# Loads of k in 1 KB runs with a GpSimd copy, and other durations in the plan of an attention and expert kernel

## The chip, the cores and the metric

The kernel runs on one core of one Trainium2 chip. Its engines are TensorE (PE in the rows, its weight loads PEld), VectorE (DVE), ScalarE (ACT), GpSimd (POOL) and SyncE (SP, which here only issues transfers). The metric is the device time of one execution in microseconds; lower is better.

## The reference

Three stages follow each other, all in float32.

```python
# 1. attention over a window of 64 positions; q, k, v are (4 batches, 8 heads, 576, 64)
scores = q @ k^T / 8, masked to 0 <= i - j < 64
attn = exp(scores - max);  attn /= sum(attn) + 1e-9
x = (attn @ v) as (2304 tokens, 512)
# 2. eight experts, each token goes to the best one
logits = x @ w_gate + modality_bias[modality_id];  e = argmax(logits)
out[token] = gate_weight * (relu(x @ w1[e]) @ w2[e])          # 512 -> 1024 -> 512
# 3. one dense layer; w_in, w_out are float64
h = out @ w_in                                                # 512 -> 2048
y = (h - tanh(h)) @ w_out
```

## The kernel before

**Stages.** The attention works on 16 head pairs (four per batch, numbered 0 to 15) of 512 positions, and on one tail unit per batch with the last 64 positions of its eight heads. For a pair, SP loads k, q and v; PE transposes k and q into PSUM (L549, L554), DVE or ACT copies them to SBUF, PE forms the scores of both heads (L642 puts the mask into the bank, L655 adds q times k), DVE takes the row maxima (L722), ACT the exponentials with their sums (L725), DVE the reciprocals (L728, L729), POOL mostly the product (L731). PE transposes the result (L680), ACT and DVE copy it out, and PE multiplies by v (L694). POOL also makes vb, a copy of v that is moved by half a tile (L478, L479), and the small kTt copies (L583).

**Routing.** After each batch a chain of small DVE operations with some PE work assigns its tokens to experts (L833 to L953). It needs the gate weights, which SP loads (L521, tile eqa) and DVE prepares (L525 to L534). Gated rows go to DRAM (L816).

**Experts.** Two units of 504 tokens are known early (after batches 0 and 2), three more when all batches are routed. Each is gathered (L1189), transposed (L1207), split into two fp32r parts (xh and xl, L1220), and goes through two layers of matmuls (L1282, then L1302), each as high times high, high times low and low times high. The weights come in 16 tiles per unit (L1233, L1239), are copied to wh and split off to wl (L1257) by DVE, the first two units' also by POOL. Beside it the float64 words of w_in and w_out are converted to float32 and split, tile by tile (L1378 to L1399 on DVE, L1393 and L1386 on POOL). From about 345 us on the dense layer runs (L1686, L1732).

**What sets the order.** Every instruction is put out by a planner, `Flow`. Each step of work is a generator that yields an `Op` with an engine (or several to choose from), a duration in us, what it waits for, a ring of buffers and a PSUM bank. The planner keeps a clock for each engine and one for the transfers (`wire`), picks what can start first, ties by priority, and writes the engines' instruction streams in that order once, at build time. At run time each engine goes through its stream in order and waits on semaphores. A changed duration moves instructions, though not what is computed. `Bag` is a set of buffers, some lent from the conversion's tiles (craw) until a given pair.

**The load of a pair.** A partition of the tile takes four neighbouring positions c of both heads h. It is laid out c, h, d so that one transposition takes both heads' 64 columns, which makes each run of the transfer one row of 64 floats (256 bytes). The two tiles of a pair live in one place of the bag qk: two of its own and three lent ones.

Of the kernel before, what the change touches and what calls it, by code (L numbers as in the profile page):

```python
# [8 lines left out]
F32 = mybir.dt.float32  # L9
# [23 lines left out]
NEARLY = 2  # L33
# [18 lines left out]
NWA = 3  # L52
DQ = 0.62
# [188 lines left out]
class Kernel:  # L242
# [132 lines left out]
    def front(self):  # L375
# [20 lines left out]
        R["qk"] = Bag(qk, [self.lend_qk() for i in range(3)], LEND - 1)  # L396
# [34 lines left out]

    def lend_qk(self):
        t = self.cv.tile([128, 1024], I32, name="craw", bufs=3).bitcast(F32)
        t = t.rearrange("p (x c h d) -> p x c h d", x=2, c=4, h=2)
        return t[:, 0], t[:, 1]

    def load_qk(self, pi, qk, qe=None):
# [4 lines left out]
        for t, src in ((k, "k"), (q, "q")):  # L442
            eng = nc.sync if src == "k" or qe is None else qe
            eng.dma_start(  # L444
                t, ap[src][b, h0 : h0 + 2, 0:512, :].rearrange("h (p c) d -> p c h d", c=4),
            )
        self.raw["qk", pi] = (q, k)

    def t_load(self):
        nc, ap, at, R = self.nc, self.ap, self.at, self.rings  # L450

        def qk(pi):
            r = yield Op(("SP", DQ if pi == 0 else 1.7), rings=[R["qk"].ask(pi)], prio=1.25 * pi - 2, wire=2.4)
# [3 lines left out]
            self.tk("qk", pi).t = r.t  # L457

        def tail(b):
            r = yield Op(("SP", 1.7), rings=[R["tl"]], prio=5 * b, wire=1.2)  # L460
# [6 lines left out]
        def v(pi):  # L467
            b, hp = divmod(pi, 4)
            h0 = 2 * hp
            r = yield Op(("SP", 1.3), rings=[R["va"]], prio=1.25 * pi + 0.3, wire=1.2)  # L470
# [11 lines left out]
        def vtail(b):  # L482
            r = yield Op(("SP", 1.3), rings=[R["vt"]], prio=5 * b + 2, wire=1.1)
# [53 lines left out]
    def t_prep(self):  # L537
        nc, R = self.nc, self.rings
        for pi in range(4 * B):
            b, hp = divmod(pi, 4)  # L540
            base = 5 * b + hp - 0.75
            q, k = self.raw["qk", pi] if ("qk", pi) in self.raw else (None, None)
            r = yield Op(("PE", 0.45), [self.tk("qk", pi)], [R["kT"].ask(pi)], bank=self.bankA | self.bankX, prio=base)
            self.raw["kTr", pi] = r.rel[0]
            self.raw["T", pi] = r.rel[0].x
            q, k = self.raw["qk", pi]
# [4 lines left out]
            r = yield Op(("PE", 0.45), bank=self.bankA | self.bankX, prio=base)  # L551
            pq, bq = self.bt(r, 128, 4, 128), r.bt
            for c in range(4):
                nc.tensor.transpose(pq[:, c, :], q[:, c].rearrange("p h d -> p (h d)"), self.idF)  # L554
            self.raw["qkr", pi].t = r.t
# [160 lines left out]
    def t_soft(self, key, ps, P, bs, tok):  # L716
# [6 lines left out]
        r = yield Op(("ACT", 1.25), [r.tok])  # L723
# [3 lines left out]
        r = yield Op(("DVE", 0.3), [r.tok])  # L727
# [97 lines left out]
    def route(self, b):  # L825
# [36 lines left out]
        r = yield Op(("DVE", 0.8))  # L862
# [172 lines left out]
    def unit_table(self, tc):  # L1035
# [29 lines left out]
        r3 = yield Op(("DVE", 3.0))  # L1065
# [181 lines left out]
    def t_wsplit(self, i, s, w, tok, rel):  # L1247
# [6 lines left out]
        by = dict(DVE=0.72, POOL=1.1) if i < NEARLY else dict(DVE=0.72)  # L1254
# [103 lines left out]
    def t_conv(self, n, t):  # L1358
        nc, cv, R = self.nc, self.cv, self.rings
        yield Op(None, [self.tk("w", *t), self.tk("O", CONV0), Tok(CONVT + CONVP * n)])  # L1360
        yield Op(None, [t for b in ("qk", "kT", "P") for t in R[b].back()])
# [524 lines left out]
```

## Time and profile before

| what | value |
|---|---|
| median of 3 runs | 765.63 us (765.39 to 768.44) |
| the profiled execution | 763.43 us, its span 761.3 us |
| busy in the span | PE 96%, DVE 83%, ACT 68%, POOL 40% |
| chain that ended last | PE 80%, DVE 9%, issue 3%, ACT 2%, DMA 2%, SP queue 2% |
| PE busy in 0 to 93 us | 78.96 of 93 us |
| PE busy in 140 to 205 us | 61.02 of 65 us |
| PE busy in 205 to 345 us | 140.00 of 140 us |

The chain that ended last is followed back from the last instruction; its shares say which engine the end waited for, summed over the whole span. The stages differ: the attention fills roughly the first 93 us, attention and the first expert units share 93 to 205 us, experts alone run to 345 us, the dense layer after that. A busy PE is not a PE at its peak, since the ends of matmuls are modelled; how long the same work takes in another stretch says more.

### The profile page before, as it was taken

How to read it: one execution, taken by the hardware profiler on the slowest of the kernel's cores; microseconds unless marked ns; L12 is line 12 of the kernel's file. 1: busy time of each engine (PE TensorE's matmuls, PEld its weight loads, DVE VectorE, ACT ScalarE, POOL GpSimd, SP SyncE). 2: the span in 40 equal slices, each digit the busy share in tenths (PEclk: the TensorE clock that was granted, in tenths of full speed). 3: DMA queues.
4: the chain of work that ended last, by engine and by line, in shares of the span. 5: the costliest groups of instructions: out<-in, count | busy, mean ns of one | idle time of the engine just before them, and what ended most of it. 6: DMA issues, size and time to landing. Idle time of an engine off the chain costs nothing.

```text
span 761.3 us, 14216 instructions
## 1 busy us (share of the span) xinstructions
PE 729.1 (96%) x4940; PEld 630.5 (83%) x4940; DVE 628.5 (83%) x1112; ACT 519.5 (68%) x1226; POOL 303.8 (40%) x322
## 2 busy tenths in 40 slices
PE   7898899999899999998999999999999999999994
PEld 4687677778688887897999989899999999898982
DVE  5799887889988978556998988888898888889883
ACT  4689777647656556448897777677767777776761
POOL 4556543233442422118694433234243324423221
PEclk9999999999999999999999999999999999999998
DMA  9989935668787774651010100001010001001001
GB/s 157 192 197 226 219 98 146 193 186 252 216 269 220 228 250 167 202 154 29 2 43 1 42 21 22 14 29 42 1 43 22 21 5 39 22 0 43 1 0 46
DMA packets 129462, 77.28 MB, mean 102 GB/s; under 512 B 67764, under 2 KB 122548, under 8 KB 129382
## 3 DMA queue, kind: packets, MB, share of 16 engines
q1 hardware_dynamic: 122502, 66.38, 32.1%
q0 software_dynamic: 3264, 9.63, 4.3%
q8 instruction: 41, 0.67, 0.4%
q10 hardware_dynamic: 3616, 0.28, 0.4%
q14 instruction: 39, 0.32, 0.1%
HBM read 62.10 MB, written 14.16 MB: 100 GB/s over the span
## 4 chain that ended last, share of the span: by engine, by line
PE 80%; DVE 9%; issue 3%; ACT 2%; DMA 2%; SPq 2%; POOL 0%; DVEq 0%; POOLq 0%; ACTq 0%
PE ps_g L1686 25%; PE ps_q L1732 25%; PE bank L1302 13%; PE bank L1282 10%; DVE wl L1257 1%; PE bank L1207 1%; PE bank L694 1%; DMA kr<-in_k 1%; PE bank L655 1%; SPq L444 1%; ACT P L725 1%; PE bank L680 1%; DMA eqa<-in_wg 1%; DVE rhs L933 1%; PE bank L833 1%
## 5 line engine op out<-in xcount | busy, mean ns | idle before, releaser
L1717 POOL TENSOR_TENSOR gl<-gv,gh 128x384 fp32r<-128x384 f32 x94 | 100.7, 1071 | 166.4 <-ACT gh L1716 166.1
L1708 DVE COPY_PREDICATED gv<-gm,gt 128x384 f32<-128x384 int32 x96 | 110.7, 1153 | 10.2 <-ACT gu L1698 0.5
L1732 PE MATMUL ps_q<-H,gl 128*128 128x512 f32 x288 | 113.3, 396 | 0.2 <-DVE gl L1717 0.2
L1732 PE MATMUL ps_q<-H,gh 128*128 128x512 f32 x288 | 113.0, 392 | 0.0
L1716 ACT ACTIVATE gh<-gv 128x384 fp32r<-128x384 f32 x96 | 50.2, 523 | 89.2 <-issue 77.8
L1704 DVE SCALAR_TENSOR_TENSOR gv<-gu,ps_g 128x384 f32<-128x384 f32 x96 | 52.9, 551 | 40.1 <-ACT gt L1701 39.6
L1706 DVE SCALAR_TENSOR_TENSOR gv<-gs,gv 128x384 f32<-128x384 f32 x96 | 77.3, 805 | 3.3
L1257 DVE TENSOR_TENSOR wl<-raw,wh 128x512 fp32r<-128x512 f32 x76 | 69.7, 933 | 10.9 <-ACT wh L368 10.1
L1732 PEld LDWEIGHTS ps_q<-H,gl 128*128 128x128 f32 x288 | 54.0, 188 | 12.7 <-DVE gl L1717 0.6
L1705 DVE SCALAR_TENSOR_TENSOR gv<-gs,gv 128x384 f32<-128x384 f32 x96 | 60.2, 627 | 3.3
L1700 ACT ACTIVATE gs<-gu,pa 128x384 f32<-128x384 f32 x96 | 57.9, 604 | 6.4 <-DVE gv L1706 6.4
L1699 ACT ACTIVATE gs<-gu,pa 128x384 f32<-128x384 f32 x96 | 59.3, 618 | 3.5 <-DVE gv L1705 0.3
L1732 PEld LDWEIGHTS ps_q<-H,gh 128*128 128x128 f32 x288 | 54.1, 188 | 8.8
L1703 ACT ACTIVATE gm<-gu,pth 128x384 f32<-128x384 f32 x96 | 58.1, 605 | 0.0
L1707 DVE TENSOR_TENSOR gt<-ps_g,gt 128x384 f32<-128x384 f32 x96 | 52.6, 548 | 0.0
L1698 ACT ACTIVATE gu<-ps_g 128x384 f32<-128x384 f32 x96 | 45.4, 473 | 0.0
L1701 ACT ACTIVATE gt<-ps_g 128x384 f32<-128x384 f32 x96 | 45.1, 470 | 0.0
L725 ACT ACTIVATE P<-bank,nm 128x128 f32<-128x128 f32 x104 | 37.3, 400 | 10.9 <-DVE nm L722 10.7
L368 ACT ACTIVATE ys<-bank 128x504 f32<-128x504 f32 (+1 forms) x20 | 11.1, 556 | 47.4 <-PE bank L1302 29.9
L1282 PE MATMUL bank<-xl,wh 128*128 128x504 f32 (+1 forms) x160 | 41.8, 378 | 0.0
L1282 PE MATMUL bank<-xh,wh 128*128 128x504 f32 (+1 forms) x160 | 40.8, 374 | 0.0
L1282 PE MATMUL bank<-xh,wl 128*128 128x504 f32 (+1 forms) x160 | 40.5, 373 | 0.0
(454 smaller groups left out, 2035.5 us busy)
## 6 DMA issues: line engine op xcount, KB each, us to landing
raw<-in_w SPq DMA_DIRECT2D x80, 256.0 KB, 4.0
craw<-in_win SPq DMA_DIRECT2D x16, 512.0 KB, 5.1
craw<-in_wout SPq DMA_DIRECT2D x16, 512.0 KB, 4.0
va<-in_v SPq DMA_DIRECT2D x32, 128.0 KB, 5.0
yd<-ys SPq DMA_DIRECT2D x16, 252.0 KB, 4.1
yr<-yd SPq DMA_DIRECT2D x20, 192.0 KB, 2.4
kr<-in_k SPq DMA_DIRECT2D x10, 256.0 KB, 4.9
qr<-in_q SPq DMA_DIRECT2D x9, 256.0 KB, 5.9
```

The costliest lines, as they stand in the source:

```text
L1257: self.eng(r).tensor_tensor(lo, w, hi.bitcast(F32), op=ALU.subtract)
L1282: nc.tensor.matmul(ps, wt[:, k, :], xt[:, k, :n], start=(k == 0 and q == 0), stop=(k == 3 and q == 2))
L1302: nc.tensor.matmul(ps, wt[:, k % 4, :], h, start=(q == 0), stop=(q == 3 * NF1 - 1))
L1686: nc.tensor.matmul(ps, w[:, c, :], x[:, c, :], start=(c == 0 and i == 0), stop=(c == 3 and i == 2))
L1699: nc.scalar.activation(s1, u, AF.Square, bias=self.pa1)
L1700: nc.scalar.activation(s2, u, AF.Square, bias=self.pa2)
L1703: nc.scalar.activation(m, u, AF.Relu, bias=self.pth)
L1705: nc.vector.scalar_tensor_tensor(v, s1, b1, v, op0=ALU.add, op1=ALU.mult)
L1706: nc.vector.scalar_tensor_tensor(v, s2, b2, v, op0=ALU.add, op1=ALU.mult)
L1708: nc.vector.copy_predicated(v, m.bitcast(I32), t)
L1717: (nc.vector if last else nc.gpsimd).tensor_tensor(gl, v, gh.bitcast(F32), op=ALU.subtract)
L1732: nc.tensor.matmul(self.po[t], g[:, t * 128 : t * 128 + 128], w, start=(f == 0 and i == 0), stop=(f == NF2 - 1 and i == 2),)
```

## The change

For k of pairs 1 to 10 (`PACK`) the transfer now writes a partition's 512 floats in the order h, c, d. A run is then four positions of one head, 256 floats or 1 KB, and the load has 256 runs in place of 1,024. GpSimd copies the tile into the order c, h, d in another tile (`t_pack`, line 465 of the changed file), and PE transposes from there. q, v, the tails and k of the other pairs stay as they were. The two buffers for the copies (bag qp) are cut from one of the three lent places of qk, which keeps two. The other edits are numbers of the plan: transfer times by run length (`W256`, `W1K`), and durations of the exponentials, of the reciprocals, of two routing steps on DVE and of the weight splits. The diff, cut to its core (where a line is changed in the same way in several places, one stands):

```diff
@@ constants
+W256, W1K = 1.34, 0.77
+PACK = {("k", pi) for pi in range(1, LEND - 1)}
@@ front()
-        R["qk"] = Bag(qk, [self.lend_qk() for i in range(3)], LEND - 1)
+        R["qk"] = Bag(qk, [self.lend_qk() for i in range(2)], LEND - 1)
+        R["qp"] = Bag([], [t.rearrange("p (c h d) -> p c h d", h=2, c=4) for t in self.lend_flat()], LEND - 1)
...
+    def lend_flat(self):
+        t = self.cv.tile([128, 1024], I32, name="craw", bufs=3).bitcast(F32)
+        return t[:, 0:512], t[:, 512:1024]
...
@@ load_qk()
-            eng.dma_start(
-                t, ap[src][b, h0 : h0 + 2, 0:512, :].rearrange("h (p c) d -> p c h d", c=4),
-            )
+            x = ap[src][b, h0 : h0 + 2, 0:512, :]
+            if (src, pi) in PACK:
+                t = t.rearrange("p c h d -> p (c h d)").rearrange("p (h c d) -> p h c d", h=2, c=4)
+                eng.dma_start(t, x.rearrange("h (p c) d -> p h c d", c=4))
+            else:
+                eng.dma_start(t, x.rearrange("h (p c) d -> p c h d", c=4))
...
+    def t_pack(self, pi, n, tok):
+        new, to = self.tk("qp", n, pi), self.raw["qk", pi]["qk".index(n)]
+        if (n, pi) in PACK:
+            r = yield Op(dict(POOL=0.8), [tok], [self.rings["qp"].ask(pi)], prio=1.25 * pi - 1)
+            x = to.rearrange("p c h d -> p (c h d)").rearrange("p (h c d) -> p c h d", h=2, c=4)
+            to = r.rel[0].x
+            self.nc.gpsimd.tensor_copy(to, x)
+        else:
+            r = yield Op(None, [tok])
+        self.raw["qp", n, pi] = to, r.rel
+        new.t = r.t
@@ t_load(): the planner's transfer times
-            r = yield Op(("SP", DQ if pi == 0 else 1.7), rings=[R["qk"].ask(pi)], prio=1.25 * pi - 2, wire=2.4)
+            r = yield Op(("SP", DQ if pi == 0 else 1.7), rings=[R["qk"].ask(pi)], prio=1.25 * pi - 2, wire=sum(W1K if (n, pi) in PACK else W256 for n in "qk"))
...
+            for n in "kq":
+                self.flow.add(self.t_pack(pi, n, r.tok), 1.25 * pi - 1)
-            r = yield Op(("SP", 1.7), rings=[R["tl"]], prio=5 * b, wire=1.2)
+            r = yield Op(("SP", 1.7), rings=[R["tl"]], prio=5 * b, wire=W256)
...
@@ t_prep(): the transposes wait for the packed tile
-            r = yield Op(("PE", 0.45), [self.tk("qk", pi)], [R["kT"].ask(pi)], bank=self.bankA | self.bankX, prio=base)
+            r = yield Op(("PE", 0.45), [self.tk("qp", "k", pi)], [R["kT"].ask(pi)], bank=self.bankA | self.bankX, prio=base)
...
-            q, k = self.raw["qk", pi]
+            k, rk = self.raw["qp", "k", pi]
...
+            for t in rk:
+                t.t = r.t
@@ planner's durations
-        r = yield Op(("ACT", 1.25), [r.tok])
+        r = yield Op(("ACT", 1.37), [r.tok])
...
-        r = yield Op(("DVE", 0.3), [r.tok])
+        r = yield Op(("DVE", 0.36), [r.tok])
...
-        r = yield Op(("DVE", 0.8))
+        r = yield Op(("DVE", 1.1))
...
-        r3 = yield Op(("DVE", 3.0))
+        r3 = yield Op(("DVE", 4.5))
...
-        by = dict(DVE=0.72, POOL=1.1) if i < NEARLY else dict(DVE=0.72)
+        by = dict(DVE=0.8, POOL=1.2) if i < NEARLY else dict(DVE=0.8)
@@ t_conv(): a lent buffer more to wait for
-        yield Op(None, [t for b in ("qk", "kT", "P") for t in R[b].back()])
+        yield Op(None, [t for b in ("qk", "qp", "kT", "P") for t in R[b].back()])
```

Since the planner writes the streams anew, instructions move on all engines. In the changed file the lines have other numbers: 465 is the new copy, 502 and 503 make vb, 549 to 558 prepare the gate, 599 and 591 copy kT and qT, 611 makes kTt, 644 copies the tail's k, 750 takes the maxima, 756 and 757 are the reciprocals, 759 is the product, 372 the copies, 1248, 1285 and 1344 make xl, wl and hl, 1406 to 1427 convert.

First place, DVE's stream around the preparation of the gate (eqa is the loaded gate weight, nm the maxima, smm and rc the sums and reciprocals, PT the transposed product). Before:

```order
L571 COPY kT_104<-bank_465 128x4x2x64
L728 TENSOR_SCALAR smm<-smm 128x4
L729 RECIPROCAL rc<-smm 128x4
L616 COPY kTt_86<-bank_496 128x4x64
L525 COPY wgp<-eqa 128x4x8
...
L534 TENSOR_TENSOR btok<-btok,ob 128x160
L722 TENSOR_REDUCE nm<-bank_535 128x4
L722 TENSOR_REDUCE nm<-bank_536 128x4
L370 COPY PT<-bank_591 128x512
```

And now:

```order
L757 RECIPROCAL rc<-smm 128x4
L644 COPY kTt_86<-bank_495 128x4x64
L372 COPY PT<-bank_508 128x512
L549 COPY wgp<-eqa 128x4x8
...
L558 TENSOR_TENSOR btok<-btok,ob 128x160
L756 TENSOR_SCALAR smm<-smm 128x4
L757 RECIPROCAL rc<-smm 128x4
L750 TENSOR_REDUCE nm<-bank_538 128x4
L750 TENSOR_REDUCE nm<-bank_539 128x4
L750 TENSOR_REDUCE nm<-bank_597 128x4
L599 COPY kT_106<-bank_613 128x4x2x64
```

The preparation keeps its place, before the maxima of pair 3. One copy of a product moved ahead of it, and one pair of reciprocals (pair 2, second head) moved behind it.

Second place, POOL's stream from the product of pair 1 to that of pair 2 (vb is the copy of v, cva and cvr are lent buffers of products). Before:

```order
L731 TENSOR_TENSOR P_113<-P_113,rc 128x512
L731 TENSOR_TENSOR P_114<-P_114,rc 128x512
L478 COPY vb<-va 64x384
L479 COPY vb<-va 64x384
L731 TENSOR_TENSOR cva<-cva,rc 128x512
L731 TENSOR_TENSOR cvr<-cvr,rc 128x512
L583 COPY kTt_86<-kT_104 128x64
```

And now, where `craw<-kr` is the new copy:

```order
L759 TENSOR_TENSOR P_113<-P_113,rc 128x512
L759 TENSOR_TENSOR P_114<-P_114,rc 128x512
L502 COPY vb<-va 64x384
L503 COPY vb<-va 64x384
L611 COPY kTt_86<-kT_104 128x64
L759 TENSOR_TENSOR cva<-cva,rc 128x512
L465 COPY craw<-kr_97 128x512
L465 COPY craw<-kr_99 128x512
L759 TENSOR_TENSOR cvr<-cvr,rc 128x512
```

The copies of k of pairs 4 and 5 stand between the two products of pair 2.

Third place, DVE's stream just ahead of the third expert unit's first xl. Before:

```order
L1378 TENSOR_SCALAR cva<-cva 128x512
L1316 SCALAR_TENSOR_TENSOR hl_133<-bank_3447,hh_125 128x504
L1257 TENSOR_TENSOR wl<-raw,wh 128x512
L1340 CAST pif<-ids_2471 126x4
L1380 TENSOR_SCALAR cva<-cva 128x512
L1382 SCALAR_TENSOR_TENSOR cva<-craw,cva 128x512
L1316 SCALAR_TENSOR_TENSOR hl_134<-bank_3474,hh_126 128x504
L1257 TENSOR_TENSOR wl<-raw,wh 128x512
L1220 TENSOR_TENSOR xl<-bank_3513,xh 128x504
```

And now:

```order
L1344 SCALAR_TENSOR_TENSOR hl_133<-bank_3415,hh_125 128x504
L1285 TENSOR_TENSOR wl<-raw,wh 128x512
L1368 CAST pif<-ids_2503 126x4
L1408 TENSOR_SCALAR cva<-cva 128x512
L1410 SCALAR_TENSOR_TENSOR cva<-craw,cva 128x512
L1344 SCALAR_TENSOR_TENSOR hl_134<-bank_3445,hh_126 128x504
L1248 TENSOR_TENSOR xl<-bank_3483,xh 128x504
```

The last split of a weight tile went behind xl. Counted from the start of the stream to that first xl, DVE has 24 weight splits and 10 converted tiles (L1378) before, and 21 and 6 now; two of the splits went to POOL, the rest comes later.

## Rows read from the trace of the kernel before

**Rows 1.** Busy time by stretch: us, engines' busy time, PE clock, DMA share, GB/s

```profile
10.00:60.00 50.00, 43.76 (x777) 35.91 (x775) 40.82 (x117) 38.11 (x162) 27.29 (x41) 0.97 0.98 195
30.00:40.00 10.00, 9.55 (x182) 8.21 (x183) 8.42 (x20) 7.68 (x38) 5.89 (x10) 0.83 1.04 197
175.00:204.00 29.00, 26.69 (x123) 21.48 (x122) 28.73 (x45) 21.20 (x40) 9.43 (x7) 1.00 0.77 223
```

**Rows 2.** Transfers of 8 to 23 us, then of 165 to 175 us

```profile
DMA packets 11881, 2.85 MB, mean 190 GB/s; under 512 B 11879, under 2 KB 11879, under 8 KB 11879
...
DMA packets 3019, 3.12 MB, mean 312 GB/s; under 512 B 176, under 2 KB 2838, under 8 KB 3018
```

**Rows 3.** SP's queue in time; issue times (ns shortest/median/longest); us to landing

```profile
21.16 1.06 SPq L521 DMA_DIRECT2D eqa<-in_wg  x1
22.88 0.61 SPq L444 DMA_DIRECT2D kr<-in_k  x1
...
L444 SPq DMA_DIRECT2D kr<-in_k x10: 607/959/4162, 0.8 to 88.8; - x10
...
L1407 SPq DMA_DIRECT2D craw<-in_win x16: 374/382/1588, 135.3 to 233.8; - x16
...
kr<-in_k SPq DMA_DIRECT2D x10, 256.0 KB, 4.9
```

**Rows 4.** DVE in order of time: start, us, line; in brackets idle time before

```profile
23.03 0.39 DVE L616 COPY kTt<-bank 128x256 f32<-128x256 f32 x1
26.44 0.18 DVE L525 COPY wgp<-eqa 128x32 f32<-128x32 f32 x1 [3.02 <-DMA eqa<-in_wg]
...
27.89 1.28 DVE L722 TENSOR_REDUCE nm<-bank 128x4 f32<-128x512 f32 x2
```

**Rows 5.** PE in order of time, from pair 4's transposes on

```profile
27.55 0.60 PE L554 MATMUL bank<-idF,craw 128*128 128x128 f32 x4
29.87 0.34 PE L694 MATMUL bank<-PT,va 128*64 128x64 f32 x4 [1.72 <-issue]
...
32.03 1.12 PE L549 MATMUL bank<-idF,kr 128*128 128x128 f32 x4
...
34.36 1.11 PE L655 MATMUL bank<-kT,qT 64*64 64x128 f32 x32
35.30 0.38 PE L642 MATMUL bank<-mF,idB 64*64 64x512 bf16 x2
...
37.12 0.66 PE L549 MATMUL bank<-idF,kr 128*128 128x128 f32 x4
```

**Rows 6.** POOL in order of time, then DVE's sums at the same time

```profile
25.49 0.24 POOL L583 COPY kTt<-kT 128x64 f32<-128x64 f32 x1
29.86 0.50 POOL L478 COPY vb<-va 64x384 f32<-64x384 f32 x1 [4.13 <-DMA va<-in_v]
...
41.45 1.04 POOL L731 TENSOR_TENSOR P<-P,rc 128x512 f32<-128x512 f32 x1 [0.77 <-DVE rc L729]
...
41.63 0.89 DVE L728 TENSOR_SCALAR smm<-smm 128x4 f32<-128x4 f32 x1 [0.32 <-ACT P L725]
```

**Rows 7.** The chain of waits, 175 to 248 us: start, us, what

```profile
175.74 2.75 PE bank L1282 x12
...
203.89 0.65 PE bank L1207 x4
...
225.91 21.97 PE bank L1282 x96
```

**Rows 8.** DVE by line, 175 to 204 us: count, busy us, mean ns

```profile
L1257 DVE TENSOR_TENSOR wl<-raw,wh 128x512 fp32r<-128x512 f32 x10 | 11.3, 1133 | 0.0
...
L1382 DVE SCALAR_TENSOR_TENSOR cva<-craw,cva 128x512 int32<-128x512 int32 x7 | 4.8, 691 | 0.2
L1380 DVE TENSOR_SCALAR cva<-cva 128x512 int32<-128x512 int32 x7 | 3.9, 559 | 0.1
L1378 DVE TENSOR_SCALAR cva<-cva 128x512 f32<-128x512 f32 x6 | 2.5, 416 | 0.0
```

More of the change, by code (lines that the diff above doesn't have):

```diff
@@ L469, in v @@
             h0 = 2 * hp
-            r = yield Op(("SP", 1.3), rings=[R["va"]], prio=1.25 * pi + 0.3, wire=1.2)
+            r = yield Op(("SP", 1.3), rings=[R["va"]], prio=1.25 * pi + 0.3, wire=W256)
             va = at.tile([128, 4, 2, 64], F32, name="va", bufs=NVA)
@@ L482, in vtail @@
         def vtail(b):
-            r = yield Op(("SP", 1.3), rings=[R["vt"]], prio=5 * b + 2, wire=1.1)
+            r = yield Op(("SP", 1.3), rings=[R["vt"]], prio=5 * b + 2, wire=W256)
             nc.sync.dma_start(self.vt, ap["v"][b, :, 448:576, :].rearrange("h p d -> p h d"))
@@ L541, in t_prep @@
             base = 5 * b + hp - 0.75
-            q, k = self.raw["qk", pi] if ("qk", pi) in self.raw else (None, None)
-            r = yield Op(("PE", 0.45), [self.tk("qk", pi)], [R["kT"].ask(pi)], bank=self.bankA | self.bankX, prio=base)
+            r = yield Op(("PE", 0.45), [self.tk("qp", "k", pi)], [R["kT"].ask(pi)], bank=self.bankA | self.bankX, prio=base)
             self.raw["kTr", pi] = r.rel[0]
             self.raw["T", pi] = r.rel[0].x
-            q, k = self.raw["qk", pi]
+            k, rk = self.raw["qp", "k", pi]
             pk, bk = self.bt(r, 128, 4, 128), r.bt
@@ L550, in t_prep @@
             self.flow.add(self.t_kcopy(pi, pk, bk, r.tok), base)
-            r = yield Op(("PE", 0.45), bank=self.bankA | self.bankX, prio=base)
+            for t in rk:
+                t.t = r.t
+            r = yield Op(("PE", 0.45), [self.tk("qp", "q", pi)], bank=self.bankA | self.bankX, prio=base)
+            q, rk = self.raw["qp", "q", pi]
             pq, bq = self.bt(r, 128, 4, 128), r.bt
@@ L554, in t_prep @@
                 nc.tensor.transpose(pq[:, c, :], q[:, c].rearrange("p h d -> p (h d)"), self.idF)
+            for t in rk:
+                t.t = r.t
             self.raw["qkr", pi].t = r.t
```

## The prediction

> **What bounds the kernel now.** I read the busy time by stretch first, then the transfers, then DVE, PE and POOL in order of time around the stalls, and last the chain of waits from 175 us on. PE does the same matmuls before and after, so what can be won is time in which PE waits or runs slowly, and that lies ahead of 204 us. Two places hold a good part of it.
>
> The first is at 22 to 36 us. Up to 60 us the transfer engines are full, at a share of 0.98 and 195 GB/s [rows 1], and from 8 to 23 us all but two of the packets are under 512 B [rows 2]. In that queue stands the gate weight, issued at 21.16 us behind the q, k and v of four pairs [rows 3]. DVE ends its work at 23.42 us and stands still for 3.02 us until that weight lands; what is queued behind it, the maxima of pair 3, starts at 27.89 us [rows 4]. PE then stands still for 1.72 us ahead of pair 2's last product, and the chip grants it a lower clock: 0.83 on average in 30 to 40 us [rows 1], so in part the lower of its two levels, 1.2 GHz in place of 2.4. Four transposes take 1.12 us at 32.03 us and 0.66 us at 37.12 us [rows 5].
>
> The second is at 175 to 204 us. PE starts the second expert unit's first layer at 175.74 us and goes on to the next unit's transposes at 203.89 us, 28.15 us later. The same 96 matmuls of the next unit take 21.97 us [rows 7]. So 6.2 us are lost, and DVE is the reason: busy for 28.73 of 29 us [rows 1], with weight splits of 1,133 ns and conversions of 416 to 691 ns [rows 8].
>
> **The change part by part.**
>
> *Ten loads of k.* A load of 256 KB takes 1.38 us at 190 GB/s. With packets mostly from 512 B to 2 KB the same engines moved 312 GB/s, that is 0.84 us [rows 2]. The difference is 0.54 us a load, and four of the ten loads stand ahead of the gate weight: 2.2 us. If SP's issuing were the pace and not the bytes, the difference would be that of the shortest issues, 0.607 against 0.374 us [rows 3], 0.9 us for four. If neither is, it is nothing. I take 2.2 us, since the engines are full there, and keep 0. The six later loads end nobody's wait that I found in these rows; I count them at nothing, hidden under loads that run well ahead of their use, and if that cover is gone each is worth its 0.5 us.
>
> The Trainium skill has another price ("DMA: Bandwidth & Descriptors", section "Why small descriptors are slow (HBM only)"): a fixed cost of about 3 cycles on top of 8 for a packet of 256 B, 27% by its words. By that alone a run of 1 KB would save about a fifth of 1.38 us, an estimate of 0.29 us a load and 1.1 us for four, and the sum below would come out about 1.1 us higher. The rows' 190 against 312 GB/s say more than that, with other packet sizes and another mix.
>
> *The gate and what is behind it.* The weight lands at 24.2 us instead of 26.44. DVE still waits for it: of what moved, one copy came ahead and one pair of reciprocals went behind, about 0.2 us in all. The preparation takes 1.45 us (26.44 to 27.89) and ends at 25.7. Behind it now come pair 2's last reciprocal and then its product on POOL. That product also stands behind two of the new copies, the second of which needs k of pair 5. This load was issued at 22.88 us, now about 2.2 us earlier, and lands 4.9 us after that [rows 3], at 25.6. So POOL starts the product at about 26.2 either way and ends at 27.2, with 1.04 us for it [rows 6]. PE then has 24 transposes and the scores of pair 4 ahead, by the pace at full clock (four transposes in about 0.5 us between starts, the scores in 0.94 us from 34.36 to 35.30 [rows 5]) some 3.1 us with the masks. Pair 4's scores end at about 30.3, against 35.30 before; most of pair 2's last product now comes after them, an estimate of 1.4 of the 2.16 us between its start at 29.87 and 32.03 us. That is 3.6 us won: 2.2 from the data, about 1 from the clock, the rest from the order. PE's wait for the product stays, so the clock may fall again: I take 3.0 us, with 0 and 3.7 as ends.
>
> *Ten copies on POOL.* The trace has no such copy. Its copies take 0.24 us for 64 elements a partition and 0.50 us for 384 [rows 6], which goes on to 0.61 us for 512; the product, with two inputs, takes 1.04. Ten copies make 6.1 us, at most 10.4. POOL is busy for 27.29 of the 50 us to 60 us [rows 1], so there is room. The copy adds its length to the way from a landed k to its transposition; where the load is early enough this costs nothing. What it can cost is DVE: the small sum at 41.63 us takes 0.89 us and ends at 42.52, together with POOL's product (41.45 plus 1.04) [rows 6]. Most of DVE's time goes to reads of PSUM, so I let two of ten copies strike, each with about 0.25 us, and take 0.5 us; the ends are 0 and 6.1.
>
> *The buffers.* One of three lent places for q and k goes, so loads run four pairs ahead instead of five. SP's next load into a place waits for the transposes of q four pairs before; pair 5 takes the place that pair 1 left. Nothing by these rows, under a microsecond if the first batch's loads stall.
>
> *The plan's durations.* They cost no time themselves; they move work. Two things are seen in the order. First, ahead of the third unit's first split DVE has 3 weight splits and 4 converted tiles less. By the means in [rows 8] that is 3.4 us plus 4 x 1.67 us, 10.1 us less. Against this stand six more copies that DVE takes over from ScalarE, 3.8 us by the 0.64 us of one maximum [rows 4], which reads as many elements. Net about 6 us less in the stretch in which DVE makes PE wait for 6.2. The removed work comes later, where PE was busy all the time and DVE had room. Second, the routing of the last batch comes later: 88 of the first unit's 96 first-layer matmuls stand ahead of it, 50 before. So its DVE chain falls between the first units' splits, which takes back a part. I take half of the 5 us that seem sure, 2.5 us, with 0 and 6.2 as ends.
>
> **The sum.** 763.43 - 3.0 - 2.5 + 0.5 = 758.4 us for an execution like the profiled one, whose span is 761.3 us with 2.1 us around it. The median of the runs shown, 765.63, lies 2.2 us above the profiled one, so the forecast for the median is 760.6 us. Rearranged work elsewhere I put at 0, give or take 1.5 us.
>
> **The rivals.**
>
> *Given back.* The early gain is real, but PE only reaches the stretch at 175 us sooner and waits there for DVE, whose stream has the routing of the last batch in it. For: DVE was busy for 28.73 of 29 us. Against: DVE too stands still for less time early on. Both terms then come to nothing but half a microsecond: 765.1 us.
>
> *Both in full.* 3.7 and 6.2 us, no lock: 755.7 us. For: the stalls stand in the rows. Against: DVE would have to be no bound anywhere.
>
> *Slower: GpSimd becomes the bound from 8 to 60 us.* Place: POOL's stream, where each copy waits for its k, and a product of probabilities or a vb waits behind it. Each vb wait of this kind was as long as 4.13 us [rows 6]. If every copy delays a product on the path by 0.61 to 1.04 us, that is 6.1 to 10.4 us, less the 2.2 us of the loads: 4 to 8 us, and a time of about 770 us. It decides from the point at which products start over 0.6 us later after their reciprocals, on average, than now. Against: POOL has 22.7 us free, and four units are in work at a time. By the Trainium skill ("SBUF — State Buffer", section "Who interferes with whom") a GpSimd instruction and certain DVE instructions exclude each other for the whole length of one, which makes the lock of up to 0.61 us a copy part of this case; the row at 41.63 us agrees.
>
> *The loads get no quicker.* What paces them is then not the packets: half a microsecond of copies on DVE, and the later stretch as it may be: 764.5 us.
>
> **How the numbers follow.** The forecast 0.43 (its own range 758.5 to 763), given back 0.24, both in full 0.12, GpSimd 0.16, loads no quicker 0.05. Half a percent, 3.8 us, is about what a measurement of this kernel tells from no change: the bounds are 761.8 and 769.5. Faster: three quarters of the forecast, the full case and a little of the third, 0.48. Slower: the GpSimd case, 0.16. Same: 0.36. The range from 755.5 to 769.5 us leaves out most of the GpSimd case and half of the full one.
>
> **What would show it.** In the profile after: the wait ahead of the gate's preparation under 1.5 us and its start before 25 us; k loads with packets of 1 KB and more than 200 GB/s until 30 us; POOL's copies near 0.6 us; the scores of pair 4 ending before 32.5 us; the second unit's first layer in under 26 us. The forecast is wrong if the gate still lands after 26 us, if PE's waits ahead of the transposes of products grow, or if the layer still takes 28 us.

## The result, and the profile after

The changed kernel took 758.46 us (median of 7 runs, 755.77 to 761.83), the kernel before 766.83 us beside it (764.91 to 768.84): a ratio of 0.9895, with an interval of 0.987 to 0.992, or 8 us. The forecast was 760.6 us, worked out from the 765.63 us of the three runs that were shown. The profiled execution took 756.57 us, its span 754.7 us, against 763.43 and 761.3 us before. PE's share of the chain that ended last rose from 80% to 88%, DVE's fell from 9% to 5%.

Busy time by stretch in the changed kernel, the columns as in [rows 1]:

```profile
10.00:60.00 50.00, 45.24 (x837) 37.31 (x836) 44.06 (x124) 42.04 (x183) 34.64 (x52) 1.00 0.92 210
30.00:40.00 10.00, 10.00 (x247) 8.20 (x240) 9.74 (x22) 8.51 (x44) 7.57 (x12) 1.00 0.88 208
175.00:204.00 29.00, 29.00 (x137) 23.76 (x136) 26.73 (x48) 19.37 (x37) 11.18 (x10) 1.00 0.81 234
```

In all three PE waits less than in [rows 1]. The granted clock in 30 to 40 us is 1.00 in place of 0.83, DVE is busy for 26.73 us of the 29 in which it was busy for 28.73, and the transfers of the first stretch run at 210 GB/s. Those of 8 to 23 us, to be held against the first of [rows 2], are in a tenth of their packets longer than 512 B and run at 212 GB/s:

```profile
DMA packets 10153, 3.18 MB, mean 212 GB/s; under 512 B 9149, under 2 KB 10149, under 8 KB 10149
```

In order of time (start, us, engine and line, in brackets the idle time before and what ended it), the gate weight, its preparation and pair 2's product, which stood in [rows 3 to 6]:

```profile
18.91 0.69 SPq L545 DMA_DIRECT2D eqa<-in_wg  x1
...
22.44 0.41 DVE L549 COPY wgp<-eqa 128x32 f32<-128x32 f32 x1 [0.33 <-DMA eqa<-in_wg]
22.77 0.60 POOL L465 COPY craw<-kr 128x512 f32<-128x512 f32 x1
22.77 0.63 DVE L551 CAST obp<-obp 128x20 f32<-128x20 int32 x1
24.22 0.33 DVE L556 TENSOR_TENSOR btok<-obp,rhs 128x160 f32<-128x160 f32 x1 [0.60 <-DMA rhs<-in_mb]
25.00 0.61 POOL L465 COPY craw<-kr 128x512 f32<-128x512 f32 x1 [1.63 <-PE bank L771]
25.05 0.58 DVE L756 TENSOR_SCALAR smm<-smm 128x4 f32<-128x4 f32 x1
25.77 1.86 DVE L750 TENSOR_REDUCE nm<-bank 128x4 f32<-128x512 f32 x3
26.00 1.04 POOL L759 TENSOR_TENSOR cvr<-cvr,rc 128x512 f32<-128x512 f32 x1 [0.38 <-DVE rc L757]
27.09 0.46 PE L708 MATMUL bank<-idF,cvr 64*128 64x64 f32 x8 [0.68 <-POOL cvr L759]
29.74 1.10 PE L683 MATMUL bank<-kT,qT 64*64 64x128 f32 x32
...
34.20 1.04 PE L683 MATMUL bank<-cvw 64*64 64x128 f32 x32
```

The weight is issued 2.25 us earlier and DVE waits for it for 0.33 us in place of 3.02. Pair 4's scores end at 30.84 us; before they ended at 35.47 (34.36 plus 1.11 [rows 5]).

The chain of waits from 171 to 246 us, which answers to [rows 7]:

```profile
171.21 7.79 PE bank L1310 x34
...
179.10 14.38 PE bank L1310 x62
...
193.94 1.29 PE bank L1235 x12
...
217.31 21.97 PE bank L1310 x96
```

This chain follows what the end waited for. It isn't a list of what PE lost, so PE's own rows have to stand beside it, before and then after:

```profile
152.73 0.65 PE L1207 MATMUL bank<-idF,xg 126*128 126x126 f32 x4 [1.67 <-DVE T L953]
...
175.57 1.07 PE L1282 MATMUL bank<-xh,wh 128*128 128x504 f32 x4
...
197.55 0.62 PE L1302 MATMUL bank<-hh,wh 128*128 128x504 f32 x2
198.00 1.45 PE L1207 MATMUL bank<-idF,xg 126*128 126x126 f32 x12
...
203.89 0.65 PE L1207 MATMUL bank<-idF,xg 126*128 126x126 f32 x4 [2.14 <-DVE xl L1220]
...
206.25 3.05 PE L1302 MATMUL bank<-hl,wh 128*128 128x504 f32 x8
```

```profile
171.05 1.07 PE L1310 MATMUL bank<-xh,wh 128*128 128x504 f32 x4
...
193.32 0.62 PE L1330 MATMUL bank<-hh,wh 128*128 128x504 f32 x2
193.77 1.46 PE L1235 MATMUL bank<-idF,xg 126*128 126x126 f32 x12
...
244.37 0.65 PE L1235 MATMUL bank<-idF,xg 126*128 126x126 f32 x4 [1.50 <-DVE xl L1248]
```

The second unit's first layer runs through in both kernels, in some 22 us, and so it does in every kernel below (22.1 to 22.6 us). What changed lies ahead of it and behind it. Before, PE waited 1.67 us for the routing's table T and 2.14 us for the next unit's xl, and after that second wait the granted clock was 0.72 in 204 to 210 us, so in part at the lower level: eight matmuls took 3.05 us there, and 2.00 at other places. Both waits are gone. The fourth unit's xl is now late instead, by 1.50 us at 244.37 us; the clock stays at 1.00 behind it. The 28.15 us of [rows 7] run to the last four of the sixteen transpositions of the next unit. Taken in this way the stretch is 28.3 us before and 25.4 now, and where an expectation below gives the length of the second unit's first layer, this stretch is meant.

**A measure for all kernels below.** All of them do the same matmuls, in different orders. So I took PE's time at a mark, less the matmuls that stand ahead of the mark in its stream at their full pace: 0.229 us for 504 columns (21.97 us by 96) and about as much for 512, 0.108 us for a transposition (1.29 us by 12), 0.03 us for the small ones. What is left is the time that PE has lost so far, good to some 0.7 us, since the prices are rough and a trace can lack some matmuls. *Front* is that loss at the first transposition of the second expert unit (some 150 us), *late* what is added until the last one of the fourth unit (some 250 us). Both are worked out from single profiled executions; the ratio is from timed runs, each against the kernel before on the same chip. On the chip of e5, e7, e8 and t_134 the kernel before took 762.41 us, on the others 766.83 to 768.48, and the changed kernel was not timed on the first; a ratio of these four and one of the others can differ by the chip alone. *Ahead* is the number of converted tiles that DVE has ahead of the third unit's first xl.

| kernel | k loads | durations | transfer times | ahead | front | late | ratio (interval) |
|---|---|---|---|---|---|---|---|
| before | 256 B | old | old | 10 | 49.8 | 6.6 | 1 |
| changed | 1 KB | new | new | 6 | 47.0 | 2.5 | 0.9895 (0.987 to 0.992) |
| e3_short_runs | 256 B | new | new | 6 | 53.6 | 2.4 | 0.9931 (0.9913 to 0.9949) |
| e4_double_copy | 1 KB, copies twice | new | new | 6 | 48.0 | 2.4 | 0.9879 (0.9862 to 0.9897) |
| e9_after_shift | 1 KB | new | new | 6 | 49.4 | 2.4 | 0.9892 (0.9871 to 0.9914) |
| e12_gather_late | 1 KB | new | new | 6 | 51.7 | 2.4 | 0.9863 (0.983 to 0.9896) |
| t_134 | 1 KB | new | new | 6 | 50.6 | 3.3 | 0.995 (0.9929 to 0.9972) |
| e11_old_wires | 1 KB | new | old | 8 | 58.4 | 3.6 | 0.9987 (0.9969 to 1.0005) |
| e10_old_durations | 1 KB | old | new | 10 | 54.4 | 7.8 | 0.9973 (0.9952 to 0.9994) |
| e2_pack_only | 1 KB | old | old | 10 | 56.2 | 7.9 | 1.0042 (1.0023 to 1.0061) |
| e8_pack_shift | 1 KB | old | old | 10 | 48.1 | 8.8 | 1.0042 (1.0025 to 1.006) |
| e1_plan_only | 256 B | new | new | 6 | 55.9 | 3.1 | 0.9994 (0.9975 to 1.0013) |
| e7_plan_shift | 256 B | new | new | 6 | 48.7 | 2.6 | 0.9962 (0.9941 to 0.9982) |
| e5_conv_late | 256 B | old | old | 6 | 49.2 | 4.4 | 1.004 (1.0024 to 1.0055) |

*Late* falls into two groups: 6.6 to 8.8 us with the old durations, 2.4 to 3.6 us with the new ones. Between them, at 4.4 us, lies e5, which has the old durations but only 6 tiles ahead. It is steady: 2.4 or 2.5 us in the five kernels with the changed kernel's streams and due times. *Front* goes from 47.0 to 58.4 us and follows no single edit. In these five it goes from 47.0 to 53.6. The profiled execution of e10_old_durations took 4.5 us more than that kernel's median, that of e11_old_wires 3.1 more, that of the changed kernel 1.9 less, so one execution can't rank fronts that are a few us apart.

### The profile page after: what moved, and what is told of

The parts are those of the page before. It is cut to its first block, busy times and chain, and to the rows that moved or that the text cites. A ratio compares the mean times of both kernels' runs of the same rounds, so it can differ in the third digit from the quotient of the medians.

```text
span 754.7 us, 14255 instructions
## 1 busy us (share of the span) xinstructions
PE 726.0 (96%) x4940; PEld 627.6 (83%) x4940; DVE 631.4 (84%) x1110; ACT 521.2 (69%) x1225; POOL 316.4 (42%) x335
## 4 chain that ended last, share of the span: by engine, by line
PE 88%; DVE 5%; issue 2%; ACT 2%; POOL 1%; DMA 1%; SPq 0%; POOLq 0%; ACTq 0%; DVEq 0%
PE ps_g L1714 26%; PE ps_q L1760 25%; PE bank L1310 14%; PE bank L1330 13%; PE bank L683 2%; PE bank L722 2%; PE bank L1235 1%; ACT P L753 1%; PE bank L708 1%; PE bank L524 1%; PE bank L833 1%; PE bank L861 1%; PE bank L670 1%; DMA rhs<-in_mb 1%; DVE nm L750 1%
## 5 line engine op out<-in xcount | busy, mean ns | idle before, releaser
L1285 DVE TENSOR_TENSOR wl<-raw,wh 128x512 fp32r<-128x512 f32 x74 | 65.4, 900 | 8.0 <-ACT wh L370 6.7
L370 ACT ACTIVATE wh<-raw 128x512 fp32r<-128x512 f32 x70 | 42.8, 630 | 1.6 <-DMA raw<-in_w 1.4
```

What stands on the lines that cost most here:

```text
L1285: self.eng(r).tensor_tensor(lo, w, hi.bitcast(F32), op=ALU.subtract)
```

## The experiments

**The run length alone (e3_short_runs).** The changed kernel with k loaded in rows, and the same copies:

```diff
-            if (src, pi) in PACK:
+            if False:
...
-            x = to.rearrange("p c h d -> p (c h d)").rearrange("p (h c d) -> p c h d", h=2, c=4)
+            x = to
```

> The changed kernel's very order, with GpSimd's ten copies, but k arrives in rows of 256 bytes, already in the order for the transposition; only the length of the runs is undone. Theory: the gate weight lands about 2 us later than with 1 KB runs, near 24.5 us, pair 4's scores end 2 to 3 us later, and the time is 2 to 3 us above the changed kernel's: ratio to before 0.993. Rival 1 (run length does nothing; SP's place in the queue and the plan do it all): same as the changed kernel, 0.989. Rival 2 (loads carry all): 1.000.

Measured: 0.9931, against 0.9895; 0.0036 of 767 us are 2.8 us, and the two intervals leave 0.4 to 5.1 us. Against the next kernel, e4, which ran on the same chip, it is 4.0 us. Its queue, DVE, POOL and PE, as shown above for the changed kernel, and the stretch of 30 to 40 us:

```profile
20.64 0.84 SPq L545 DMA_DIRECT2D eqa<-in_wg  x1
...
24.86 0.18 DVE L549 COPY wgp<-eqa 128x32 f32<-128x32 f32 x1 [2.13 <-DMA eqa<-in_wg]
...
27.47 0.62 POOL L465 COPY craw<-kr 128x512 f32<-128x512 f32 x1 [2.69 <-DMA kr<-in_k]
29.14 0.46 PE L708 MATMUL bank<-idF,cvr 64*128 64x64 f32 x8 [2.12 <-POOL cvr L759]
...
31.35 1.98 PE L683 MATMUL bank<-kT,qT 64*64 64x128 f32 x32
...
37.27 1.04 PE L683 MATMUL bank<-cvw 64*64 64x128 f32 x32
```

```profile
30.00:40.00 10.00, 9.88 (x190) 8.38 (x192) 9.28 (x21) 7.57 (x38) 6.55 (x11) 0.83 1.09 182
```

With every instruction in the same order, short runs bring the weight 2.4 us later (24.86 against 22.44), DVE waits 2.13 us again, and the clock of 0.83 is back. PE, whose stream is the same in both, comes to the scores of the next pair 3.07 us later (37.27 against 34.20). The theory holds, and the size is that of the prediction's early term. But the gate isn't the only way by which the run length acts: with short runs pair 2's product waits last for the copy of pair 5's k, which starts when that load lands and ends at 28.09 us, 0.6 us after the reciprocal behind the gate. With 1 KB runs that copy had ended at 25.61 us, ahead of the reciprocal at 25.85.

**The price of the copies (e4_double_copy).**

```diff
             self.nc.gpsimd.tensor_copy(to, x)
+            self.nc.gpsimd.tensor_copy(to, x)
```

> The changed kernel's order with each of GpSimd's ten copies done twice, 6.1 us more work on GpSimd. Theory (copies are mostly covered): 0.3 to 1.5 us above the changed kernel, ratio to before 0.990 to 0.991. Rival (a copy stands on the path with its length, so that the packed loads gain more than is seen and pay it back): about 6 us above the changed kernel, ratio 0.997.

Measured: 0.9879, no slower than the changed kernel, and below the 0.990 to 0.991 of the theory. Ten copies more, 6.1 us of work, cost nothing that shows, which rules out the rival's 0.997. So the ten that the change adds are covered in the main as well; a cost of half a microsecond would not show in these runs.

**The plan's numbers alone, and the loads alone (e1_plan_only, e2_pack_only).** The first is the kernel before with the two changes of numbers:

```diff
-        r = yield Op(("ACT", 1.25), [r.tok])
+        r = yield Op(("ACT", 1.37), [r.tok])
...
-            r = yield Op(("SP", 1.7), rings=[R["tl"]], prio=5 * b, wire=1.2)
+            r = yield Op(("SP", 1.7), rings=[R["tl"]], prio=5 * b, wire=1.34)
```

> The plan's numbers alone, on the kernel before: k in rows of 256 bytes, no copies, three lent places. Theory (two gains in two places, of which the plan's is the one at 175 to 204 us): about 5 us faster than before, ratio 0.993, since 80 of 96 matmuls stand ahead of the last routing and 6 converted tiles and 23 splits ahead of the third unit's first xl (10 and 24 before); the second unit's first layer takes 23 us in place of 28; but the gate weight still lands near 26 us. Rival 1 (all of the gain comes from the shorter loads): ratio 1.000, layer 27 us or more. Rival 2 (all of it comes from the plan): ratio 0.989, and pair 4's scores end by 32.5 us here too.

The second is the changed kernel with these numbers put back, except that of a packed load:

```diff
-        r = yield Op(("ACT", 1.37), [r.tok])
+        r = yield Op(("ACT", 1.25), [r.tok])
...
-            r = yield Op(("SP", 1.7), rings=[R["tl"]], prio=5 * b, wire=W256)
+            r = yield Op(("SP", 1.7), rings=[R["tl"]], prio=5 * b, wire=1.2)
```

> Loads of 1 KB runs and GpSimd's copies, with the durations and the other transfer times that the plan had before; the planner still counts 0.77 us for a packed load. Theory: the gate weight lands near 24 us or sooner and pair 4's scores end about 4 us earlier than before, but with 10 converted tiles and 23 splits ahead of the third unit's first xl the second unit's first layer still takes 25 us or more, so that 2 to 4 us are left at the end: ratio 0.995 to 0.997. Rival 1 (the loads carry all of it): 0.989. Rival 2 (the plan carries all): 1.000, or slower by the copies.

Measured: 0.9994 and 1.0042. My theory of two gains that add up fell with both. In the second kernel DVE starts the gate's preparation at 22.49 us, as early as in the changed one, but in its profile nothing of that gain is left by 150 us: the front is 6.4 us worse than before. Behind that *late* is 1.3 us worse, with the third unit's xl late by the same 2.15 us (2.14 before), and the transposes behind it run slowly:

```profile
211.56 0.85 PE L1235 MATMUL bank<-idF,xg 126*128 126x126 f32 x4 [2.15 <-DVE xl L1248]
```

In the first kernel the relief came (late 3.1). Pair 4's scores end at 32.31 us in it, 3.2 us earlier than before, though its gate weight is there only at 25.51 us; so that mark alone does not speak for the loads. By 150 us, though, the front was 6 us worse than before. There DVE stood twice with its inputs there, for as long as GpSimd issued the four gathers of an expert unit. The second time:

```profile
128.64 1.04 POOL L1189 DMA_INDIRECT xg<-xs,ids  x1 [0.18 <-issue]
...
132.59 0.99 POOL L1189 DMA_INDIRECT xg<-xs,ids  x1 [0.30 <-issue]
...
133.56 1.29 DVE L722 TENSOR_REDUCE nm<-bank 128x4 f32<-128x512 f32 x2 [4.17 <-remote]
133.57 0.40 PE L694 MATMUL bank<-PT,va 128*64 128x64 f32 x3 [0.39 <-remote]
```

"remote" is the profile's word for a releaser that it doesn't know. The scores that DVE was to read were done by 130.49 us.

**Shifting VectorE's stream (e7_plan_shift, e8_pack_shift, e9_after_shift).** Is it the place of the instruction in the stream? The same edit in the numbers-only, the loads-only and the changed kernel:

```diff
-        nc.vector.memset(self.pth, -TAU2)
+        for i in range(25): nc.vector.memset(self.pth, -TAU2)
```

> The kernel with the plan's numbers alone, and 24 more tiny VectorE memsets at the start, where VectorE waits for the first loads; no other instruction moves. In the run without them VectorE stood for 3.47 us at 71.28 us and for 4.17 us at 133.56 us with its inputs there, each time until GpSimd's four gathers were issued. Theory (an instruction at a fixed position of VectorE's stream can't start while the gathers are issued; with 24 instructions ahead the position falls outside them): both stalls go or shrink under 1 us, PE keeps its clock in 128 to 142 us, and the time falls by 3 to 7 us, to a ratio to before of 0.990 to 0.996. Rival (the stall belongs to what VectorE does there, or to the gathers' traffic, not to the position): both stalls stay and the ratio stays at 0.999.

> The kernel with the packed loads alone, and the same 24 tiny memsets at VectorE's start. In the run without them VectorE stood for 4.39 us at 129.29 us while GpSimd issued its four gathers, PE then waited 3.59 us and its granted clock was 0.64 in 128 to 135 us. Theory (position in the stream): that stall goes, and the time falls by 4 to 7 us, ratio to before 0.995 to 0.999. Rival (not the position): it stays, ratio 1.004.

> The changed kernel with 24 more tiny VectorE memsets at the start and nothing else moved, as in the two shifted kernels before. In the changed kernel's profile VectorE did not stand while the gathers were issued, ScalarE did for 3.90 us at 67.43 us. Theory (VectorE's place in its stream is no cause of the changed kernel's time): same as the changed kernel, ratio 0.988 to 0.991. Rival (the changed kernel gained because its streams happen to fall well, and 24 instructions ahead undo that): ratio above 0.994, with a stall of VectorE of 3 to 4 us during the gathers.

In both profiles the stalls went, and with them the clock came back; the numbers-only kernel before and after the edit:

```profile
60.00:80.00 20.00, 17.72 (x303) 13.78 (x304) 12.98 (x34) 13.51 (x64) 11.38 (x16) 0.81 0.87 210
120.00:140.00 20.00, 18.60 (x197) 14.73 (x195) 13.68 (x33) 11.27 (x43) 10.18 (x9) 0.91 0.42 126
```

```profile
60.00:80.00 20.00, 17.29 (x388) 14.03 (x387) 18.05 (x56) 17.46 (x72) 12.81 (x18) 0.99 1.01 212
120.00:140.00 20.00, 20.00 (x228) 15.37 (x230) 13.92 (x30) 10.23 (x41) 8.59 (x8) 1.00 0.50 147
```

But the timed runs agree only in part: 0.9962 against 0.9994 for the numbers (the intervals touch), 1.0042 against 1.0042 for the loads, 0.9892 against 0.9895 for the changed kernel. The members of the first two pairs also ran on different chips. So nothing here shows that the stall of 4.39 us in the loads-only profile made that kernel slow (the theory had 0.995 to 0.999 without it), and whether the place in the stream decides stays open. What e8's one profile shows is a pay-back: its front is 1.7 us better than before, its late part 2.2 us worse, with PE's wait for xl at 203.11 us again 2.15 us. In the third kernel the gain of the change survives the shift, so it doesn't hang on this place in DVE's stream.

**One part of the numbers at a time (e10_old_durations, e11_old_wires).** From the changed kernel, five durations put back (one shown), or four transfer times:

```diff
-        r = yield Op(("ACT", 1.37), [r.tok])
+        r = yield Op(("ACT", 1.25), [r.tok])
```

> The changed kernel with the five durations of the plan (exponentials, reciprocals, two routing steps, splits) as they were before; packed loads, copies and the new transfer times stay. VectorE then has 24 splits and 10 converted tiles ahead of the third unit's first xl (21 and 6 in the changed kernel, 24 and 10 before). Theory (the loads' gain is paid back where VectorE is full, unless the durations thin it out there): the first unit's transposes start some 4 us earlier than before, the second unit's first layer still takes 27 us or more, ratio 0.996 to 1.000. Rival (the transfer times and the loads carry the gain): ratio 0.990.

```diff
-            r = yield Op(("SP", 1.7), rings=[R["tl"]], prio=5 * b, wire=W256)
+            r = yield Op(("SP", 1.7), rings=[R["tl"]], prio=5 * b, wire=1.2)
```

> The changed kernel with the other loads' transfer times as the plan had them before (1.2 and 1.1 us); packed loads, copies and the five durations stay. VectorE has 25 splits and 8 converted tiles ahead of the third unit's first xl, a place between the changed kernel and the one before. Theory: about half of the relief, the second unit's first layer 24 to 26 us, ratio 0.992 to 0.995. Rival (the durations alone make the difference, the transfer times none): 0.990.

Measured: 0.9973, as the theory had it (though the first unit's transposes start only 2.4 us earlier than before, not 4), and 0.9987, where it had 0.992 to 0.995. Both ran on the chip of e9, which has the changed kernel's 0.9892 there. With the old durations both waits that PE had before in 150 to 204 us are back, for the routing's table T and for xl:

```profile
159.52 0.65 PE L1235 MATMUL bank<-idF,xg 126*128 126x126 f32 x4 [2.07 <-DVE T L981]
...
209.69 0.91 PE L1235 MATMUL bank<-idF,xg 126*128 126x126 f32 x4 [2.14 <-DVE xl L1248]
```

With the old transfer times neither is (PE waits 1.61 us for hl at 165.57 us), and in the profile the loss sits in the front. In 60 to 80 us PE is busy for 14.81 us at a clock of 0.76, where the changed kernel has 16.61 at 1.00:

```profile
60.00:80.00 20.00, 14.81 (x268) 11.52 (x260) 12.47 (x31) 14.43 (x61) 10.89 (x14) 0.76 0.80 191
```

DVE stood there for 4.01 us and ACT for 3.60 us during the gathers. But t_134, whose streams up to some 105 us are the changed kernel's, has only 12.47 us at 0.82 in the same stretch of its profile. How much of the 0.0092 between this kernel and the changed one is such stalls, and how much a worse order, one profile doesn't tell.

**The conversions alone (e5_conv_late), and later still (t_134).**

```diff
-CONVT, CONVP = 122.0, 5.1
+CONVT, CONVP = 142.0, 5.1
```

> The kernel before with one number changed: converted tiles of w_in and w_out become due 20 us later, so that VectorE has 6 of them, not 10, ahead of the third unit's first xl. Nothing moves before 105 us. Theory (VectorE makes PE wait at 175 to 204 us): the second unit's first layer takes about 24 us in place of 28, and 1.5 to 3 us are left at the end, ratio 0.996 to 0.998. Rival (the relief there is given back at the next unit's xl): ratio 1.000.

```diff
-CONVT, CONVP = 122.0, 5.1
+CONVT, CONVP = 134.0, 5.1
```

> The changed kernel with the converted tiles due 12 us later (134 in place of 122), aimed at PE's new wait of 1.50 us for xl at 244 us: 16 converted tiles ahead of the fourth unit's first xl in place of 18, 26 in place of 28 ahead of the fifth's. Theory: that wait goes, 1 to 2 us below the changed kernel, ratio to before 0.987 to 0.988. Rival (VectorE has no room later either, and the wait returns at the fifth unit or at the dense layer): same as the changed kernel, 0.989, or above.

Both missed. In e5 the wait for xl went (late 4.4 in place of 6.6) as the theory has it, while that for T was there with 2.29 us. The tiles were then wanted elsewhere. The hand-over to the dense layer grew; its chain now goes through a transfer and GpSimd:

```profile
340.79 0.42 ACT ys L368
...
341.65 2.52 DMA xr<-yd
...
344.79 1.01 POOL yl L1176
```

The dense layer reached its steady pace at 363.09 us, and at 356.39 us before. So the place of the conversions frees the stretch but isn't free by itself. In t_134 the waits for xl came to 1.32 us at 201.48 us and 0.86 at 248.84, no less than the 1.50 that they were to replace. Its ratio of 0.995 can't be held against the changed kernel's 0.9895, measured where the kernel before took 766.83 us and not 762.41; the medians of the two are the same 758.46 us.

**GpSimd's wait for the gathers (e12_gather_late).** The copy that makes the second half of vb carries a wait for the gathers issued ahead of it. In two kernels whose streams agree up to some 105 us, the changed one and t_134, that wait was 3.83 and 7.18 us; the latter:

```profile
67.33 1.00 POOL L1217 DMA_INDIRECT xg<-xs,ids  x1 [0.30 <-issue]
68.33 0.52 POOL L502 COPY vb<-va 64x384 f32<-64x384 f32 x1
76.03 0.50 POOL L503 COPY vb<-va 64x384 f32<-64x384 f32 x1 [7.18 <-DMA xg<-xs,ids]
```

So I held the gathers of the first unit back until GpSimd's first weight split:

```diff
-            nc.gpsimd.indirect_dma_start(
+            go = lambda j=j: nc.gpsimd.indirect_dma_start(
...
+            self.held.append(go) if i == 0 else go()
...
         self.eng(r).tensor_tensor(lo, w, hi.bitcast(F32), op=ALU.subtract)
+        if r.e == "POOL" and len(self.held) == 4:
+            while self.held:
+                self.held.pop(0)()
```

> The changed kernel with GpSimd's four gathers of the first expert unit moved back in GpSimd's stream, behind two copies of v, three products and a weight split (some 7 us later); every other engine's stream stays as it is. In the changed kernel's profile GpSimd stood for 3.83 us behind these gathers until they had landed (7.18 us in the kernel with the conversions later, whose streams up to there are the same), and PE was busy for only 2.97 and 2.91 of 4 us in 60 to 64 and 64 to 68 us. Theory (the products behind that wait hold PE up): PE's loss in 60 to 76 us shrinks, the first unit's transposes start before 85.9 us, and the time is 1 to 3 us below the changed kernel, ratio to before 0.985 to 0.988. Rival (the wait only moves to the next copy of v, and what stands behind it there is as urgent): same as the changed kernel, 0.989, or slower.

```profile
79.83 1.02 POOL L503 COPY vb<-va 64x384 f32<-64x384 f32 x1
84.49 0.50 POOL L504 COPY vb<-va 64x384 f32<-64x384 f32 x1 [3.64 <-DMA xg<-xs,ids]
```

The wait only moved to the next vb, as the rival has it, and the first unit's transposes start at 85.68 us in place of 85.92. The ratio of 0.9863 has an interval that takes in the changed kernel's; its median of 759.52 us is no better. Not told apart.

## Why the prediction was right, and where it was not

The time lies in the range and 2.1 us from the forecast. The gain is further from it: 5.0 us were forecast and 8.4 measured. As a time it looks closer, since the kernel before took 1.2 us more beside the changed one than in the runs that the forecast starts from. In the profiles the two terms can be seen apart. Of the 6.9 us that PE has won by the fourth unit, 2.8 are front and 4.1 late, and all of it is kept: the dense layer reaches its steady pace at 349.47 us, and at 356.39 before. That the total came out close is luck in part, as the last points show.

- *Ten loads of k*, taken at 2.2 us until the gate weight: 2.4 us by the pair that differs in the run length alone, 0.6 us a load where I had 0.54 from bytes and rates. By the Trainium skill's price ("DMA: Bandwidth & Descriptors", section "Why small descriptors are slow (HBM only)") I had an estimate of 0.29 us a load beside it; the runs go against it here.
- *The gate and what is behind it*, taken at 3.0 us: 2.8 us by the timed pair, and 3.07 us at the next pair's scores in the profiles of that pair. The 2.8 us in the front are the sum of all edits up to 150 us, so that this figure is the same is chance. The steps came in order: the product started at 26.00 us (forecast 26.2) and ended at 27.04 (27.2), pair 4's scores ended at 30.84 (30.3). Two errors inside nearly cancelled. The weight came sooner than my 24.2 us, at 22.44, since the new order alone, with short runs, already brings it to 24.86 us (26.44 before). And the preparation took 2.61 us (22.44 to 25.05) where I had 1.45: DVE waited 0.60 us in it for another small load (rhs), and the cast beside a copy at 22.77 us took 0.63 us.
- *Ten copies on POOL*: nine took 0.60 to 0.61 us, as extrapolated from 64 and 384 elements, the tenth 1.46 us at 51.93 us. The half microsecond that I took for DVE's locked sums is too small to be seen in the timed runs; doubling the copies cost nothing. The lock itself is in the rows: the sum at 25.05 us takes 0.58 us beside a copy from 25.00 to 25.61, where such sums take 0.16 us alone, and the product waits for the reciprocal behind it. This is as the Trainium skill ("SBUF — State Buffer", section "Who interferes with whom") lets expect. The longer sums, of up to 1.06 us at 37.91 us, end with one of POOL's products, as the one at 41.63 us before [rows 6].
- *The plan's durations*, taken at 2.5 us: 4.1 us, and the stretch was misread. The 6.2 us "lost" were 28.15 us less the layer's 96 matmuls. But PE does 10 second-layer matmuls and 12 transpositions in it as well, 3.6 us at full pace, and [rows 1] have it busy for 26.69 of the 29 us. The layer itself took as long before as it does now, some 22 us; DVE made PE wait for xl alone, 2.14 us, and not for 6.2. The 4.1 us are made up otherwise: that wait, the 1.67 us for T at 152.73 us, which I had not read, some 1.6 us of lower clock behind the wait for xl (20 matmuls in 6.2 us in place of 4.6), less the new 1.50 us at 244.37 us. What held was the direction: 10 converted tiles ahead of xl cost PE 2.14 or 2.15 us at xl in all four such kernels, 6 or 8 at most 1.32. By e5 the tiles alone bring 2.2 of the 4.1 us. The step that halved the term was wrong too: the routing of the last batch "falls between the first units' splits, which takes back a part". It took back nothing. With 88 matmuls ahead of it PE had work until T was there; before, with 50, it waited.
- *The transfer times*, to which I gave no price of their own: this is the step that is missing. Put back alone they cost 0.0092 of the time, 7 us, of which 1.1 are late (3.6 against 2.5), so that most must lie in the front; the durations put back alone cost 0.0078, 6 us, of which 5.3 are late (7.8 against 2.5). I had looked at the two places that I knew and taken the rest of the new order to be as good as the old, give or take 1.5 us; the fronts in the table lie 11 us apart.
- *The sum* treated the edits as terms that add up. They don't: the numbers alone give 0 to 3 us, the loads alone lose 3 us, both give 8. One part is shown: with the old durations and the packed loads *late* is 1.2 to 2.2 us worse than before, in three kernels, so the rival "given back" is in part what happens without the new ones. That the rest is the planner's new order in the front is argued from the table, not shown. A sum of two terms that do not add up, without a term for a part worth 7 us, came close to the total by luck.
- *GpSimd becomes the bound* is out: POOL was busy for 34.64 us of 50 and, with the copies doubled, for 38.79, with no loss of time.

## What to carry to other kernels

Where a planner writes the order from durations, a change of a load and of the durations that describe it is one change: read each stretch for what ends last there, and don't price a part as if the order of the rest stayed. A gain early in the kernel can be lost at the next engine that is full, as in e8, unless that engine is thinned out too. The chain that ended last says what the end waited for; what an engine lost in a stretch stands in that engine's own rows, with all the work that it does there. One profile of a front with many short dependent steps can be 8 us off another of nearly the same code, so such parts are judged by timed runs.

## What the runs showed that was not expected

While GpSimd issues four gathers (some 5 us, 128.64 to 133.58 us in the numbers-only kernel), DVE or ACT can stand for 1.4 to 4.7 us with nothing to wait for that the profile knows; it happened in nine of the fourteen profiled kernels, not in before. PE then drips as well: in the numbers-only kernel its small matmuls came in batches of 5 or 6 every 0.74 to 0.76 us from 131.33 to 133.57 us. Behind it the granted clock falls, to 0.81 in 60 to 80 us there and 0.75 in the kernel with the old durations. The changed kernel has such a stall too (ACT, 3.90 us at 67.43 us), but its clock stays at 1.00 up to 140 us. What holds the engines is open.
